# One set of convolution taps, another W_in order, and W_out through the SyncE ring

## The chip, the cores and the metric

One NeuronCore of one Trainium2 chip runs the whole program. The metric is device microseconds of one execution, lower is better. Each time is a median of several executions, with their lowest and highest value. "The span" is the length of the one execution that the profiler recorded, without the launch; times inside an execution count from the span's start. A "station" is the time of a named event in it, such as the first W_out matmul; a transfer has "landed" when its last completion signal arrives.

## The reference

A lightweight causal convolution (7 taps per head, softmax over the taps), followed by a feed-forward block with exact GELU:

```python
x: (8, 4096, 192) fp32, weight: (8, 7)         # 8 heads of 24 channels
w = softmax(weight, axis=-1)
y[b, s, 24*h + g] = sum_k w[h, k] * x[b, s - 6 + k, 24*h + g]   # zero before s = 0
x2 = y.reshape(32768, 192)
out = gelu(x2 @ w_in) @ w_out                   # (192, 2048), then (2048, 192)
```

## The kernel before

The 32768 tokens are two halves of 16384; half 0 lives on partitions 0 to 63, half 1 on 64 to 127. A "third" is 64 of the 192 channels (every third channel), so three thirds side by side hold a token's channels. Tiles are of 256 tokens per half at first (six of them), then of 512. A tile is loaded and transposed on VectorE; tiles 0 and 1 are convolved on TensorE (diagonal matrices times a bf16 copy of x), later tiles on VectorE. Then TensorE does x times W_in, ScalarE the GELU, and TensorE, one tile behind, GELU times W_out. The W_in work is done in units: the matmuls of one unit feed one GELU, and a slice of W_out matmuls stands between two units. The "halo" is the six tokens before a tile, which the convolution needs and GpSimd copies.

Cut to what the change touches (cuts marked):

```python
# GpSimd: identity mask first, then W_in in three pieces with a cast to bf16
g.wait_ge(S_MSET, 1)
... affine_select -> idb ...
for i in range(3):
    win_in(FP[i], FP[i + 1], S_WIN[i])
... halo(0) ...
g.dma_start(wout, W_out).then_inc(S_WOUT, 16)     # one transfer, casts to bf16
halo(1)

# VectorE: taps and diagonals, one set for each third
v.tensor_copy(wch, wnt with each head repeated 24 times)
for q in range(4):
    v.transpose(wcol[quarter q], wch ...)         # 32 x 96
def diag(p): v.tensor_tensor(dg[third p], idb, wcol[third p], ALU.mult)
diag(0); diag(1)                                  # third 2 is made on ScalarE
for p in range(NP): trans(0, p)                   # tile 0
dup(0)                                            # copy a W_in piece to the other 64 partitions
conv_out(v, 0, 1); conv_out(v, 0, 4)
dup(1); dup(2)
for p in range(NP): trans(1, p)                   # tile 1
for p in range(NP): cast(1, p)                    # fp32 -> bf16 for TensorE

# ScalarE
a.wait_ge(S_WARM, 1)                              # VectorE's memset of the warm-up tile
a.activation(out=hot, in_=warm, func=AF.Exp)
load(a, 0, (2, 3))                                # half of tile 0 of x
... softmax ...
for k in range(KS): a.activation(out=dg[third 2, tap k], in_=idb, func=AF.Copy, scale=wcol)
for p in range(NP): a.activation(out=xTb[0], in_=xT[0], func=AF.Copy)   # bf16 copy of tile 0

# TensorE
for i in range(16): t.matmul(hp[1], warm, warm)   # warm-up
... convolution of tile 0, then of tile 1 behind units 4 and 5 of tile 0 ...

# SyncE
load weight; load(sp, 0, (0, 1))                  # the other half of tile 0 of x
sp.wait_ge(S_WIN[0], 32)
load(sp, 1); load(sp, 2)
sp.wait_ge(S_WOUT, 16); load(sp, 3)
```

Of the kernel before, what the change touches and what calls it, by code (L numbers as in the profile page):

```python
# [11 lines left out]
def bass_lightweight_conv__then__act_gelu_exact_kernel(  # L12
# [36 lines left out]
    HX = 8  # L49
# [36 lines left out]
    CH = []  # L86
    for s in range(4):
        CH += [2 * s, 2 * s + 1, NF // 2 + 2 * s, NF // 2 + 2 * s + 1]
# [21 lines left out]
    with es:  # L110
# [9 lines left out]
        wch = sbt("wch", [32, D], F32)  # L120
        wcol = sbt("wcol", [128, NP * 32], F32)
        idb = sbt("idb", [128, 64], BF16)
        dg = sbt("dg", [128, NP * KS * 64], BF16)
# [14 lines left out]
        S_WOUT = sem("S_WOUT")  # L138
# [13 lines left out]
        S_DGA = sem("S_DGA")  # L152
# [55 lines left out]
        FP = [0, FQ, 2 * FQ, FH]  # L208

# [163 lines left out]
        def _(g):  # L373
# [6 lines left out]

            g.wait_ge(S_MSET, 1)
# [11 lines left out]
            for i in range(3):  # L393
                win_in(FP[i], FP[i + 1], S_WIN[i])

            def halo(n):
# [45 lines left out]
            g.dma_start(  # L442
                ap(wout, 0, [[NF * C, 128], [2 * C, NF // 2], [1, 2 * C]]),
                ap(woutt, 0, [[2 * C, 128], [256 * C, NF // 2], [1, 2 * C]]),
            ).then_inc(S_WOUT, 16)
            halo(1)
            for n in range(2, NB):
                halo(n)

        @block.vector  # L450
        def _(v):
# [16 lines left out]

            v.wait_ge(S_PRO, 4)
            v.transpose(wnt[:, :], wnm[:, :]).then_inc(S_PRO)  # L470
            v.wait_ge(S_PRO, 5)
            v.tensor_copy(
                ap(wch, 0, [[D, 32], [GRP, H], [1, GRP]]),
                ap(wnt, 0, [[32, 32], [1, H], [0, GRP]]),
            ).then_inc(S_PRO)
            v.wait_ge(S_PRO, 6)
            for q in range(4):
                v.transpose(
                    ap(wcol, 32 * q * NP * 32, [[NP * 32, 32], [1, NP * 32]]),
                    ap(wch, DQ * (q % 2), [[D, 32], [1, NP], [NP, 32]]),  # L480
                ).then_inc(S_PRO)
            v.wait_ge(S_PRO, 10)
            v.wait_ge(S_IDN, 2)

            def diag(p):
                v.tensor_tensor(
                    ap(dg, p * KS * 64, [[NP * KS * 64, 128], [64, KS], [1, 64]]),
                    ap(idb, 0, [[64, 128], [0, KS], [1, 64]]),
                    ap(wcol, p * 32, [[NP * 32, 128], [1, KS], [0, 64]]),
                    ALU.mult,  # L490
                ).then_inc(S_DG)
# [17 lines left out]

            def cast(n, p):  # L510
                v.wait_ge(S_TR, NP * n + p + 1)
                v.tensor_copy(
                    ap(xTb[PC[n]], p * XB + HX, [[NP * XB, 128], [1, WS[n]]]),
                    ap(xT[n % 2], p * XW + HX, [[NP * XW, 128], [1, WS[n]]]),
                ).then_inc(S_CAST[PC[n]])
# [21 lines left out]
            def conv(n, k, p):  # L537
# [13 lines left out]
                wk = wcol[:, p * 32 + kt : p * 32 + kt + 1]  # L551
# [30 lines left out]
            diag(0)  # L582
            diag(1)
            for p in range(NP):
                trans(0, p)
            dup(0)
            conv_out(v, 0, 1)
            conv_out(v, 0, 4)
            dup(1)
            dup(2)  # L590
            for p in range(NP):
                trans(1, p)
            for p in range(NP):
                cast(1, p)
# [21 lines left out]
        def _(a):  # L616
            a.wait_ge(S_WARM, 1)
            a.activation(out=hot[:, 0:1], in_=warm[0:1, 0:1], func=AF.Exp).then_inc(S_ACTP)
# [10 lines left out]
            a.activation(out=hot[:, 1:2], in_=warm[0:1, 0:1], func=AF.Gelu).then_inc(S_HOT)  # L629
            a.wait_ge(S_PRO, 10)  # L630
            a.wait_ge(S_IDN, 2)
            for k in range(KS):
                d0 = ((NP - 1) * KS + k) * 64
                c0 = (NP - 1) * 32 + k
                a.activation(
                    out=dg[:, d0 : d0 + 64],
                    in_=idb[:, :],
                    func=AF.Copy,
                    scale=wcol[:, c0 : c0 + 1],
                ).then_inc(S_DGA)  # L640
# [288 lines left out]
```

## Time and profile before

| | before |
|---|---|
| time, median of 3 runs | 684.32 us (683.9 to 684.7) |
| span of the profiled run | 682.0 us |
| TensorE busy | 676.2 us (99%) |
| VectorE / ScalarE / GpSimd busy | 82% / 79% / 5% |
| first W_out matmul | 19.24 us |
| from that matmul to the end | 662.8 us |

### The profile page before, as it was taken

The numbers are of one execution on the slowest core, as the hardware profiler recorded it, in microseconds if no ns is written. First come the engines' busy times: TensorE is split into PE (matmuls) and PEld (weight loads), VectorE is DVE, ScalarE is ACT, GpSimd is POOL, SyncE is SP. The second block draws the span as 40 slices with busy tenths as digits, with TensorE's granted clock in tenths as the row PEclk, the third lists the DMA queues.
The fourth block names the chain that finished last, engine by engine and source line by source line (L and its number), as shares of the span: only waits on it lengthen the run. The fifth ranks groups of instructions, "written<-read, shape, count | busy, mean of one in ns | idle before, by whom it ended". The sixth has DMA issues, their size and how long they took to land.

```text
span 682.0 us, 27319 instructions
## 1 busy us (share of the span) xinstructions
PE 676.2 (99%) x12576; PEld 407.5 (60%) x12576; DVE 562.2 (82%) x909; ACT 538.4 (79%) x557; POOL 35.1 (5%) x51
## 2 busy tenths in 40 slices
PE   8999999999999999999999999999999999999998
PEld 4899655555555555555555555555555555555556
DVE  7899979888889888899888898888898888988611
ACT  7899988777787777787777788777778777778772
POOL 4026100000000000000000000000000000000000
PEclk9999999999999999999999999999999999999999
DMA  9345322134432143332234322334422434310223
GB/s 178 77 107 130 83 60 72 44 78 95 95 94 54 45 94 94 95 77 52 63 94 95 94 68 45 80 94 96 94 53 46 95 94 96 82 43 21 48 49 94
DMA packets 132946, 54.00 MB, mean 79 GB/s; under 512 B 126432, under 2 KB 132704, under 8 KB 132832
## 3 DMA queue, kind: packets, MB, share of 16 engines
q1 hardware_dynamic: 129872, 49.93, 31.5%
q0 software_dynamic: 2288, 1.57, 1.6%
q8 instruction: 98, 1.61, 1.0%
q10 hardware_dynamic: 672, 0.76, 0.4%
q14 instruction: 16, 0.13, 0.1%
HBM read 28.66 MB, written 25.17 MB: 79 GB/s over the span
## 4 chain that ended last, share of the span: by engine, by line
PE 97%; ACT 2%; issue 0%; DVE 0%
PE hp L774 47%; PE ob L838 43%; PE ob L805 6%; ACT gT L694 2%; PE hp L708 1%; PE ob L727 0%; ACT xc L192 0%; ACT osb L261 0%; DVE osb L303 0%; DVE osb L272 0%; DVE warm L452 0%
## 5 line engine op out<-in xcount | busy, mean ns | idle before, releaser
L694 ACT ACTIVATE gT<-hp 128x1024 bf16<-128x1024 f32 x512 | 522.8, 1023 | 129.3 <-PE hp L774 126.0
L774 PE MATMUL hp<-xc,win 64*64 64x512 bf16 (+2 forms) x6048 | 418.9, 366 | 1.5 <-ACT gT L694 0.7
L838 PE MATMUL ob<-gT,wout 64*64 64x512 bf16 x5376 | 366.3, 376 | 0.0
L561 DVE SCALAR_TENSOR_TENSOR acc<-xT,wcol,acc 128x512 f32<-128x512 f32 (+1 forms) x495 | 314.6, 700 | 0.5 <-ACT acc L667 0.5
L774 PEld LDWEIGHTS hp<-xc,win 64*64 64x64 bf16 (+1 forms) x6048 | 187.7, 106 | 136.3 <-ACT gT L694 2.5
L838 PEld LDWEIGHTS ob<-gT,wout 64*64 64x64 bf16 x5376 | 172.2, 118 | 122.9
L303 DVE STREAM_TRANSPOSE osb<-ob 128x512 f32<-128x512 f32 x84 | 74.2, 886 | 100.8 <-PE ob L838 100.8
L528 DVE STREAM_TRANSPOSE xT<-xin 128x512 f32<-128x512 f32 (+1 forms) x105 | 78.7, 803 | 2.1 <-DMA xin<-in_x_dram 2.1
L561 DVE SCALAR_TENSOR_TENSOR xc<-xT,wcol,acc 128x512 bf16<-128x512 f32 (+1 forms) x99 | 65.3, 717 | 0.0
L438 POOL COPY xT<-xT 128x18 f32<-128x18 f32 x30 | 27.9, 930 | 515.3 <-DVE xT L528 492.3
L805 PE MATMUL ob<-wout,gT 64*128 64x192 bf16 x1024 | 52.2, 243 | 0.3
L805 PEld LDWEIGHTS ob<-wout,gT 64*128 64x128 bf16 x1024 | 43.5, 94 | 6.4 <-PE ob L805 0.6
L554 DVE TENSOR_SCALAR acc<-xT,wcol 128x512 f32<-128x512 f32 (+1 forms) x90 | 37.6, 474 | 1.1
L274 ACT ACTIVATE osb<-ob 128x192 f32<-128x192 f32 x4 | 1.3, 330 | 9.5 <-PE ob L805 9.5
L272 DVE COPY osb<-ob 128x192 f32<-128x192 f32 x4 | 1.4, 357 | 8.4 <-PE ob L805 8.4
L708 PE MATMUL hp<-warm 128*128 128x512 bf16 x16 | 6.3, 581 | 1.3 <-DVE warm L452 1.3
L261 ACT ACTIVATE osb<-ob 128x384 f32<-128x384 f32 x12 | 5.8, 487 | 0.0
L667 ACT ACTIVATE acc<-xT,wcol 128x256 f32<-128x256 f32 (+1 forms) x9 | 5.2, 575 | 0.0
L708 PEld LDWEIGHTS hp<-warm 128*128 128x128 bf16 x16 | 2.1, 139 | 4.9 <-issue 3.6
L194 DVE CAST xc<-ob 64x256 bf16<-64x256 f32 (+3 forms) x8 | 2.8, 358 | 1.6 <-PE ob L727 1.4
L376 POOL DMA_DIRECT2D win<-in_moe_w_in_dram x6 | 3.9, 653 | 0.0
L497 DVE COPY win<-win 64x768 bf16<-64x768 bf16 (+1 forms) x6 | 3.1, 509 | 0.2
(33 smaller groups left out, 21.7 us busy)
## 6 DMA issues: line engine op xcount, KB each, us to landing
out_dram<-osb SPq DMA_DIRECT2D x122, 192.0 KB, 3.1
xin<-in_x_dram SPq DMA_DIRECT2D x116, 192.0 KB, 4.1
xin<-in_x_dram SPq DMA_DIRECT2D x20, 96.0 KB, 3.2
wout<-in_moe_w_out_dram POOLq DMA_DIRECT2D x1, 768.0 KB, 11.0
win<-in_moe_w_in_dram POOLq DMA_DIRECT2D x4, 96.0 KB, 4.2
win<-in_moe_w_in_dram POOLq DMA_DIRECT2D x2, 192.0 KB, 4.8
out_dram<-osb SPq DMA_DIRECT2D x8, 48.0 KB, 1.7
out_dram<-osb ACTq DMA_DIRECT2D x4, 96.0 KB, 1.9
```

The costliest lines, as they stand in the source:

```text
L261: e.activation(out=dst, in_=src, func=AF.Copy).then_inc(S_EVA)
L303: v.transpose(ap(osb[m % 2], j, [[8 * C, 128], [C // 2, TB // 32], [NP, 32]]), bank(ring(m, j)),).then_inc(S_EV)
L438: g.tensor_copy(dst, src).then_inc(S_HALO)
L528: v.transpose(ap(xT[n % 2], p * XW + HX, [[NP * XW, 128], [1, w]]), ap(xin[n % NX], p, [[TB // 32 * DQ, 128], [D if n == 0 else DQ, w // 3 ...
L554: ins = v.tensor_scalar(a, src, wk, None, ALU.mult)
L561: ins = v.scalar_tensor_tensor(dst, src, wk, a, op0=ALU.mult, op1=ALU.add)
L667: a.activation(out=acc[n % 2][:, p * TB : p * TB + w], in_=ap(xT[n % 2], p * XW + HX, [[NP * XW, 128], [1, w]]), func=AF.Copy, scale=wcol[ ...
L694: a.activation(out=ap(gT[n % 2], i * c * 2 * w, dst), in_=ap(hp[u % 2], 0, src), func=AF.Gelu,).then_inc(S_GELU)
L708: t.matmul(hp[1][:, 0:512], warm[:, 0:128], warm[:, :])
L774: ins = t.matmul(hp[u % 2][fo : fo + fw, o : o + w], ap(win, f1, [[NP * F, 64], [2, fw]]), xc[n % 2][r, p * TB : p * TB + w], start=(p == ...
L805: ins = t.matmul(bank(bb[sub], w=C), gT[m % 2][r, c0 : c0 + 128], wout[r, CH[i] * C : (CH[i] + 1) * C], start=(ph == 0 and i == 0), stop=( ...
L838: ins = t.matmul(bank(ring(m, j), slice(64 * h, 64 * h + 64), w), ap(wout, 64 * hf * NF * C + CH[i] * C + j, [[NF * C, 64], [NP, 64]],), g ...
```

## The change

The intent is to shorten the start. One set of taps and diagonals for all thirds (a head has 24 channels, a multiple of 3, so channel number j of every third belongs to the same head), each token half begins with its own part of W_in, and W_out comes as fp32 in the SyncE ring and is cast on GpSimd. The diff cut to its core:

```diff
 # taps: the channel order lets all thirds use one column set
-    v.tensor_copy(wch ...); 4 x v.transpose(32 x 96); diag(0); diag(1); 7 ScalarE products
+    4 x v.transpose(32 x 32); 1 x v.tensor_tensor(dg, idb, wcol)

 # ScalarE: the first activation no longer reads the warm-up tile
-    a.wait_ge(S_WARM, 1)
-    a.activation(out=hot[:, 0:1], in_=warm[0:1, 0:1], func=AF.Exp)
+    a.activation(out=hot[:, 0:1], in_=const zero, func=AF.Exp)
     load(a, 0, (2, 3))

 # W_in order: half hf uses W_in chunks 8*hf, 8*hf+1, ... so its own partitions come first
-    CH = [0, 1, 8, 9, 2, 3, 10, 11, ...]          # the same for both halves
+    CH = [[(8 * hf + i) % NF for i in range(NF)] for hf in range(2)]
-    if n == 0 and i in (0, 2, 4): wait S_WIN[i // 2] and S_DUPE >= 2 * (i // 2) + 2
+    if n == 0 and i < 3:      wait S_WIN[i]
+    if n == 0 and 4 <= i < 7: wait S_DUPE >= 2 * (i - 4) + 2

 # GpSimd: first W_in piece ahead of the identity mask; casts move here
+    win_in(FP[0], FP[1], S_WIN[0])
     ... identity mask ...
-    for i in range(3): win_in(...)
+    for i in range(1, 3): win_in(...)
     halo(0)
-    g.dma_start(wout <- W_out, cast).then_inc(S_WOUT, 16)
     halo(1)
+    for p in range(NP): cast(g, 1, p)             # was on VectorE
+    for i in range(4):
+        g.wait_ge(S_WOUT[i], 16)
+        g.tensor_copy(wout[quarter i], woutf[quarter i]).then_inc(S_WOG)

 # SyncE
     load(sp, 1)
+    for i in range(4): sp.dma_start(woutf[quarter i] <- W_out).then_inc(S_WOUT[i], 16)
     load(sp, 2)
-    sp.wait_ge(S_WOUT, 16)
     load(sp, 3)

 # VectorE: conv_out(0) before dup(0); dup(2) after the transposes of tile 1
 # TensorE: share of W_out work behind tile 1's units: [3, 4, 4, ...] -> [4, 8, 8, 8, 9, ...]
```

More of the change, by code (lines that the diff above doesn't have):

```diff
@@ L81, in bass_lightweight_conv__then__act_gelu_exact_kernel @@
         EVC.append(EVC[n] + (0 if n < NA else NP if new else NG[n]))
-    CH = []
-    for s in range(4):
-        CH += [2 * s, 2 * s + 1, NF // 2 + 2 * s, NF // 2 + 2 * s + 1]
+    CH = [[(8 * hf + i) % NF for i in range(NF)] for hf in range(2)]
     assert all(WS[n] == TB for n in range(M0, NB))
@@ L119, in bass_lightweight_conv__then__act_gelu_exact_kernel @@
         wnt = sbt("wnt", [32, 32], F32)
-        wch = sbt("wch", [32, D], F32)
-        wcol = sbt("wcol", [128, NP * 32], F32)
+        wcol = sbt("wcol", [128, 32], F32)
+        woutf = sbt("woutf", [128, NF * C], F32)
         idb = sbt("idb", [128, 64], BF16)
-        dg = sbt("dg", [128, NP * KS * 64], BF16)
+        dg = sbt("dg", [128, KS * 64], BF16)
         warm = sbt("warm", [128, 512], BF16)
@@ L137, in bass_lightweight_conv__then__act_gelu_exact_kernel @@
         S_WIN = [sem("S_WIN%d" % i) for i in range(3)]
-        S_WOUT = sem("S_WOUT")
+        S_WOUT = [sem("S_WOUT%d" % i) for i in range(4)]
+        S_WOG = sem("S_WOG")
         S_XIN = [sem("S_XIN%d" % i) for i in range(NX)]
@@ L151, in bass_lightweight_conv__then__act_gelu_exact_kernel @@
         S_PCA = sem("S_PCA")
-        S_DGA = sem("S_DGA")
         S_DUPE = sem("S_DUPE")
@@ L208, in bass_lightweight_conv__then__act_gelu_exact_kernel, with cast @@
         FP = [0, FQ, 2 * FQ, FH]
+        WG = [0, 4, 2, 6]
+        def cast(e, n, p):
+            e.wait_ge(S_TR, NP * n + p + 1)
+            e.tensor_copy(
+                ap(xTb[PC[n]], p * XB + HX, [[NP * XB, 128], [1, WS[n]]]),
+                ap(xT[n % 2], p * XW + HX, [[NP * XW, 128], [1, WS[n]]]),
+            ).then_inc(S_CAST[PC[n]])
         def cvd(n):
@@ L392, in _ @@
                 ).then_inc(S_IDN)
-            for i in range(3):
+            for i in range(1, 3):
                 win_in(FP[i], FP[i + 1], S_WIN[i])
@@ L441, in _ @@
             halo(0)
-            g.dma_start(
-                ap(wout, 0, [[NF * C, 128], [2 * C, NF // 2], [1, 2 * C]]),
-                ap(woutt, 0, [[2 * C, 128], [256 * C, NF // 2], [1, 2 * C]]),
-            ).then_inc(S_WOUT, 16)
             halo(1)
+            for p in range(NP):
+                cast(g, 1, p)
+            for i in range(4):
+                g.wait_ge(S_WOUT[i], 16)
+                o = 2 * WG[i] * C
+                g.tensor_copy(wout[:, o : o + 4 * C], woutf[:, o : o + 4 * C]).then_inc(S_WOG)
             for n in range(2, NB):
@@ L471, in _ @@
             v.wait_ge(S_PRO, 5)
-            v.tensor_copy(
-                ap(wch, 0, [[D, 32], [GRP, H], [1, GRP]]),
-                ap(wnt, 0, [[32, 32], [1, H], [0, GRP]]),
-            ).then_inc(S_PRO)
-            v.wait_ge(S_PRO, 6)
             for q in range(4):
                 v.transpose(
-                    ap(wcol, 32 * q * NP * 32, [[NP * 32, 32], [1, NP * 32]]),
-                    ap(wch, DQ * (q % 2), [[D, 32], [1, NP], [NP, 32]]),
+                    wcol[32 * q : 32 * q + 32, :],
+                    ap(wnt, 4 * (q % 2), [[32, 32], [1, 4], [0, 8]]),
                 ).then_inc(S_PRO)
-            v.wait_ge(S_PRO, 10)
+            v.wait_ge(S_PRO, 9)
             v.wait_ge(S_IDN, 2)
-            def diag(p):
-                v.tensor_tensor(
-                    ap(dg, p * KS * 64, [[NP * KS * 64, 128], [64, KS], [1, 64]]),
-                    ap(idb, 0, [[64, 128], [0, KS], [1, 64]]),
-                    ap(wcol, p * 32, [[NP * 32, 128], [1, KS], [0, 64]]),
-                    ALU.mult,
-                ).then_inc(S_DG)
+            v.tensor_tensor(
+                ap(dg, 0, [[KS * 64, 128], [64, KS], [1, 64]]),
+                ap(idb, 0, [[64, 128], [0, KS], [1, 64]]),
+                ap(wcol, 0, [[32, 128], [1, KS], [0, 64]]),
+                ALU.mult,
+            ).then_inc(S_DG)
             def dup(s):
@@ L508, in dup @@
                     ).then_inc(S_DUPE)
-            def cast(n, p):
-                v.wait_ge(S_TR, NP * n + p + 1)
-                v.tensor_copy(
-                    ap(xTb[PC[n]], p * XB + HX, [[NP * XB, 128], [1, WS[n]]]),
-                    ap(xT[n % 2], p * XW + HX, [[NP * XW, 128], [1, WS[n]]]),
-                ).then_inc(S_CAST[PC[n]])
             def trans(n, p):
@@ L550, in conv @@
                 src = ap(xT[n % 2], p * XW + HF + kt, [[NP * XW, 128], [1, w]])
-                wk = wcol[:, p * 32 + kt : p * 32 + kt + 1]
+                wk = wcol[:, kt : kt + 1]
                 a = acc[n % 2][:, p * TB : p * TB + w]
@@ L580, in run @@
                     conv(*op[1:])
-            diag(0)
-            diag(1)
             for p in range(NP):
                 trans(0, p)
-            dup(0)
             conv_out(v, 0, 1)
             conv_out(v, 0, 4)
+            dup(0)
             dup(1)
-            dup(2)
             for p in range(NP):
                 trans(1, p)
-            for p in range(NP):
-                cast(1, p)
+            dup(2)
             for j in range(len(PIECES)):
@@ L616, in _ @@
         def _(a):
-            a.wait_ge(S_WARM, 1)
-            a.activation(out=hot[:, 0:1], in_=warm[0:1, 0:1], func=AF.Exp).then_inc(S_ACTP)
+            a.activation(
+                out=hot[:, 0:1], in_=nc.const_aps.tensor(0.0, (1, 1), F32), func=AF.Exp
+            ).then_inc(S_ACTP)
             load(a, 0, (2, 3))
@@ L628, in _ @@
             ).then_inc(S_ACTP)
-            a.activation(out=hot[:, 1:2], in_=warm[0:1, 0:1], func=AF.Gelu).then_inc(S_HOT)
-            a.wait_ge(S_PRO, 10)
-            a.wait_ge(S_IDN, 2)
-            for k in range(KS):
-                d0 = ((NP - 1) * KS + k) * 64
-                c0 = (NP - 1) * 32 + k
-                a.activation(
-                    out=dg[:, d0 : d0 + 64],
-                    in_=idb[:, :],
-                    func=AF.Copy,
-                    scale=wcol[:, c0 : c0 + 1],
-                ).then_inc(S_DGA)
+            a.activation(
+                out=hot[:, 1:2], in_=nc.const_aps.tensor(0.0, (1, 1), F32), func=AF.Gelu
+            ).then_inc(S_HOT)
+            a.wait_ge(S_PRO, 9)
             for p in range(NP):
@@ L670, in first_tap @@
                     func=AF.Copy,
-                    scale=wcol[:, p * 32 + KS - 1 : p * 32 + KS],
+                    scale=wcol[:, KS - 1 : KS],
                 ).then_inc(S_K0)
@@ L715, in pconv @@
                     if n == 0:
-                        if p < NP - 1:
-                            t.wait_ge(S_DG, p + 1)
-                        else:
-                            t.wait_ge(S_DGA, KS)
+                        t.wait_ge(S_DG, 1)
                 if k == KS - 2:
@@ L724, in pconv @@
                     r = slice(64 * hf, 64 * hf + 64)
-                    d0 = (p * KS + k) * 64
+                    d0 = k * 64
                     x0 = p * XB + (32 * k if n == 0 else HF + k) + c0
@@ L759, in mm1 @@
                         t.wait_ge(S_CV, cvd(n))
-                if n == 0 and i in (0, 2, 4):
-                    t.wait_ge(S_WIN[i // 2], 32)
-                    t.wait_ge(S_DUPE, 2 * (i // 2) + 2)
+                if n == 0 and i < 3:
+                    t.wait_ge(S_WIN[i], 32)
+                if n == 0 and 4 <= i < 7:
+                    t.wait_ge(S_DUPE, 2 * (i - 4) + 2)
                 for cc in range(c):
-                    f0 = 256 * (CH[i * c + cc] // 2) + CH[i * c + cc] % 2
                     for p in range(NP):
@@ L769, in mm1 @@
                             r = slice(64 * hf, 64 * hf + 64)
+                            ch = CH[hf][i * c + cc]
+                            f0 = 256 * (ch // 2) + ch % 2
                             fw = 64 if M0 < n <= M1 else 128
@@ L807, in mm2 @@
                         gT[m % 2][r, c0 : c0 + 128],
-                        wout[r, CH[i] * C : (CH[i] + 1) * C],
+                        wout[r, CH[sub][i] * C : (CH[sub][i] + 1) * C],
                         start=(ph == 0 and i == 0),
@@ L814, in mm2 @@
                     ins.then_inc(S_MM2 if ph == 1 else S_PH)
-            share = {1: [3, 4, 4, 4, 4, 4, 4, 4]}
+            share = {1: [4, 8, 8, 8, 9, 9, 9, 9]}
             def mm2_t(m, ps, i):
@@ L841, in mm2_t @@
                                 wout,
-                                64 * hf * NF * C + CH[i] * C + j,
+                                64 * hf * NF * C + CH[h][i] * C + j,
                                 [[NF * C, 64], [NP, 64]],
@@ L872, in _ @@
                     a1 = len(todo) * sum(ws[: i + 1]) // sum(ws)
-                    if n == 1 and a0 == 0 and a1 > 0:
-                        t.wait_ge(S_WOUT, 16)
                     for un in todo[a0:a1]:
+                        if n == 1 and un in ((0, 0, 0), (0, 0, 4)):
+                            t.wait_ge(S_WOG, 2 + un[2] // 2)
                         (mm2_t if new else mm2)(n - 1, *un)
@@ L889, in _ @@
             load(sp, 1)
+            for i in range(4):
+                g = WG[i]
+                sp.dma_start(
+                    ap(woutf, 2 * g * C, [[NF * C, 128], [2 * C, 2], [1, 2 * C]]),
+                    ap(woutt, 256 * g * C, [[2 * C, 128], [256 * C, 2], [1, 2 * C]]),
+                ).then_inc(S_WOUT[i], 16)
             load(sp, 2)
-            sp.wait_ge(S_WOUT, 16)
             load(sp, 3)
```

## The prediction

0.09 + 0.08, about 0.2 us, and 0.2 for an early clock bring 684.3 to 683.9. The second 0.2 was the author's estimate: the profile of before shows one time at which the warm-up becomes fast, 6.8 us. That W_in's first piece could hold up x of tile 0 by 0.7 us is an estimate too. It assumes that the piece gets half the turns, which was not shown: the trace of before has W_in's packets from 4.85 us on, the last of x until 5.55 us (the 5.2 and 5.9 of the prediction), and those x packets take 0.32 to 0.42 us each, the earlier ones of the same queue 0.22 to 0.41. That VectorE could shut GpSimd out rests on the one copy of 3.56 us.

> **What bounds the kernel now.** I read the chain that ended last first, since it says which engine a saved microsecond has to come from.
>
> ```profile
> PE 97%; ACT 2%; issue 0%; DVE 0%
> PE hp L774 47%; PE ob L838 43%; PE ob L805 6%; ACT gT L694 2%; PE hp L708 1%; PE ob L727 0%; ACT xc L192 0%; ACT osb L261 0%; DVE osb L303 0%; DVE osb L272 0%; DVE warm L452 0%
> ```
>
> TensorE is the path for 97% of a 682.0 us span; GELU on ScalarE is there for 2%, VectorE for nothing. The two big matmul groups (x times W_in, GELU times W_out) are 90%. To see where the rest lies I took busy time by stretch. In 30 to 350 us TensorE is busy 319.87 of 320.00 us, in 350 to 670 us 319.85 of 320.00. From 18.5 to 30 us it is 11.36 of 11.50. So nothing after 18.5 us can be won by removing a wait; the change touches no matmul count or shape there. What is left is the start, so I read the chain in order of time (start us, length us, what):
>
> ```profile
> 1.26 6.32 PE hp L708 x16
> 7.58 0.90 PE ob L727 x22
> 8.48 0.02 issue
> 8.50 0.38 ACT xc L192
> ...
> 9.94 0.63 PE hp L774 x8
> 10.57 0.02 issue
> 10.59 1.94 ACT gT L694 x2
> 12.53 0.01 issue
> 12.54 1.03 ACT gT L694
> 13.57 0.05 issue
> 13.62 0.83 PE hp L774 x12
> 14.45 0.89 PE ob L727 x28
> ...
> 17.43 1.03 ACT gT L694
> 18.46 0.05 issue
> 18.51 0.83 PE hp L774 x12
> 19.34 0.58 PE ob L805 x12
> ```
>
> This is the whole argument. The start is a relay: 16 warm-up matmuls (to 7.58), the convolution of tile 0 on TensorE, four copies on ScalarE (8.50 to 9.89), then eight GELUs of about 1.02 us, which bound the stretch from 10.59 to 19.48 us together with the convolution of tile 1 that sits between them. From the seventh GELU's end (18.46) the matrix engine runs without a break. A microsecond counts only if that moment, or the wait just after it, moves.
>
> The diagonal, tap and transpose work on VectorE is beside the warm-up, as its timeline shows (start, busy us, engine, line):
>
> ```profile
> 3.68 0.25 DVE L472 COPY wch<-wnt 32x192 f32<-32x192 f32 x1
> 3.96 1.28 DVE L478 STREAM_TRANSPOSE wcol<-wch 32x96 f32<-32x96 f32 x4
> 5.28 1.16 DVE L486 TENSOR_TENSOR dg<-idb,wcol 128x448 bf16<-128x448 bf16 x2
> 6.36 1.34 DVE L528 STREAM_TRANSPOSE xT<-xin 128x256 f32<-128x256 f32 x3
> ```
>
> [...] the warm-up matmuls start 0.427 us apart until 6.77 us, then 0.216 us apart; the last is issued at 7.20 and is done about 7.42. [...] this point may move between executions, which is part of the noise. [...] in the trace the GpSimd packets begin at 5.2 us while the last x packets of tile 0 are still going (they end at 5.9)[...]. [...] a GpSimd copy of 128x18 takes 0.22 to 0.31 us alone, but the one that begins at 39.37 us, in a run of scalar_tensor_tensor, took 3.56 us.
>
> **The change, part by part.**
>
> *One set of taps and diagonals.* Removed on VectorE: the 0.28 us wch step (3.68 to 3.96). Four transposes of 32x96 in 1.28 us become 32x32; the one of that size at 3.45 took 0.20, so about 0.8 for four. One of the two 0.58 us diagonal products goes. Sum: 0.28 + 0.48 + 0.58 = 1.3 us, so VectorE could transpose tile 0 at about 5.0 instead of 6.36. Seven ScalarE products (1.78 us, ending about 7.06) go too. But the packets of x for tile 0 end at 5.93, so the transpose begins at about 6.05 at best: 0.3 us won there. From the first transpose to the first convolution matmul took 7.51 - 6.36 = 1.15 us, so TensorE could begin at 7.2. The warm-up holds it until about 7.42. Of 1.3 us saved only 7.51 - 7.42 = 0.09 us reaches the path. The convolution's own pace (0.107 us per tap) and ScalarE's four copies behind it stay.
>
> *Each half begins with its own W_in.* The duplicates are now needed at the fifth unit instead of the first. In the kernel before, the first duplicates (7.73 to 8.60) were already done before the first GELU matmul at 9.34, so this frees nothing on the path; worth 0. The second and third pieces of W_in are wanted at units 1 and 2 (10.6 and 11.7 us); their packets ended at 7.98 and 10.07, so no new wait. W_in's first issue moves ahead of the identity mask, from 1.83 to about 0.8 us, as GpSimd waited there for VectorE. That lets tile 1 of x be issued about 0.9 us earlier (it waits for that piece)[...].
>
> *W_out through SyncE.* In the kernel before it was issued at 8.17 on GpSimd, took 11.0 us, and landed at 19.2: exactly when TensorE wanted it. The first W_out weight load at 19.24 is put down to that DMA. The switch cost 19.24 - 18.51 = 0.73 us where the next such one cost 20.40 - 19.75 = 0.65: 0.08 us lost, which the change wins back. The new transfers sit behind tile 1 in the ring, so with about 0.45 us per issue they start near 8 to 10 us. The source bytes are unchanged; a 768-byte-out packet took 84 ns, 1024 of them over 16 engines 5.4 us, so all should land by 15 to 16. Casts on GpSimd, estimated: a 128x186 cast took 0.34 and a 128x18 one 0.22, so 0.7 ns per element, and 0.75 us for 128x768 undisturbed; scaling the slowest (0.457 for 186) gives 1.9. Two casts are wanted at 19.2, all four at 20.5. With tile 1's casts done by about 13.5 even four slow ones end at 21; with normal ones, 17. I take them as in time.
>
> *Tile 1's cast from VectorE to GpSimd.* About 0.4 to 0.6 us each for 128x256 instead of 0.22. The convolution of tile 1 cannot issue before the third GELU ends (13.57) and the fifth unit's matmuls are done (14.45). If tile 1 of x lands nearer 11 than 12.2, the casts end by 13.5. Hidden.
>
> *Fewer W_out units in tile 1's first slice.* The same 64, moved later; GELU has slack there. Zero.
>
> Sum: 0.09 + 0.08 = about 0.2 us on the path out of 684.3. I add 0.2 for executions where the clock rises earlier, so that the full shortening of VectorE's prologue (up to 0.3) shows: 683.9 us.
>
> **The rivals.** *x of tile 0 becomes the wait.* W_in's packets now begin near 4.2 instead of 5.2[...]. If W_in's first piece (384 packets of 60 ns, 1.4 us over 16 engines) gets half the turns, x lands up to 0.7 us later, at about 6.6, and the convolution begins at 7.8: 0.3 us slower than now, 684.6. Against it: single x packets of 0.35 to 0.4 us grew no longer while W_in ran beside them. *GpSimd is late.* If VectorE's duplicates and convolution shut it out, the casts or the halo of tile 2 behind them slip; TensorE would wait at 20 us or for tile 2's convolution at about 29.8. VectorE ends that at 28.77, only 1 us ahead. For: the 3.56 us copy. Against: tile 2's x arrives sooner without the old W_out beside it (VectorE idled 1.72 us for it until 19.39), and the long two-input series begins only at 21.56. That would cost 1 to 2 us: 685 to 686. *The whole 1.3 us shows.* Only if warm-up were not the limit; then 683.0. The chain's first piece speaks against it.
>
> **Range and chances.** The three runs span 0.8 us, the net effect lies between -1.0 and +0.7 in most cases: 683.0 to 684.9. A 2% step is 13.7 us, more than the entire ramp before steady state could give, and no late wait could cost that: faster 0.005, same 0.985, slower 0.01.
>
> **What would show it.** Warm-up still first in the chain, with the first convolution matmul at 7.4 to 7.5 and the first GELU at 10.5; the seventh GELU ending near 18.4; VectorE's tile 0 transposes waiting for the x DMA; no W_out wait at the first W_out matmul, and GpSimd's four casts ended by 19. Wrong if a convolution matmul waits for a GpSimd cast, if W_out's matmuls wait for GpSimd, or if TensorE's steady pace after 30 us differs.

## The result, and the profile after

The changed kernel took 683.62 us (683.38 to 684.2, 4 runs); the kernel before, with one run more, 684.11 us (683.87 to 684.7, 4 runs). The ratio is 0.9993 with a 95% interval of 0.9976 to 1.001. A ratio here is the mean time of one kernel's fast runs over the mean of the other's fast runs of the same rounds, so not quite the ratio of the two medians. The forecast, 683.9 in 683.0 to 684.9, holds, and an effect of this size is not resolved from the scatter by the timed runs alone. Repeated on another chip with five rounds (run c1) it was 683.58 against 683.75 us, ratio 0.9998 (0.9985 to 1.001): there the medians differ by 0.17 us, not 0.49.

The profiles are finer than the timer here. The chain that ended last, in order of time, of the changed kernel (start us, length us, what):

```profile
1.64 4.27 DMA xin<-in_x_dram
...
5.93 0.53 DVE xT L526
...
6.55 0.43 ACT xTb L630
...
7.02 0.97 PE ob L711 x18
...
8.01 0.39 ACT xc L191
...
10.10 1.94 ACT gT L681 x2
...
16.93 1.03 ACT gT L681
...
18.01 0.83 PE hp L760 x12
18.84 0.33 PE ob L791 x8
```

Set beside the chain of before, every station from the first GELU to the last lies 0.49 or 0.50 us earlier: 10.10 for 10.59, 16.93 for 17.43, 18.01 for 18.51. The chain now starts with the loading of x and goes through VectorE's transpose and ScalarE's cast; the warm-up is no longer on it. VectorE in the same stretch (start, busy us, engine, line, in brackets the idle time before and what ended it):

```profile
3.69 0.90 DVE L485 STREAM_TRANSPOSE wcol<-wnt 32x32 f32<-32x32 f32 x4
4.62 0.63 DVE L491 TENSOR_TENSOR dg<-idb,wcol 128x448 bf16<-128x448 bf16 x1
5.93 1.33 DVE L526 STREAM_TRANSPOSE xT<-xin 128x256 f32<-128x256 f32 x3 [0.68 <-DMA xin<-in_x_dram]
```

The taps now end at 5.25 us and VectorE stands idle 0.68 us for x. The three tap rows of before ended at 6.44.

The first W_out matmul came 0.56 us earlier (18.68 for 19.24), but the span fell by 0.43 us (682.04 to 681.61, to two decimals from the packed traces): the rest is given back later. From the first W_out matmul to the end it is 662.93 us, against 662.80 before. The place is tile 2; the chain of before, then that of the changed kernel:

```profile
29.76 0.66 PE hp L774 x12
```

```profile
29.22 0.79 PE hp L760 x12
...
30.67 0.65 PE hp L760 x12
```

The first W_in unit of tile 2 (29.22) takes 0.79 instead of the 0.65 of the next: I put this down to VectorE, whose convolution of tile 2 began late (next fence) and ended at 29.03, because x of tile 2 landed at 19.62 us (19.36 before); a2 below names the wait.

```profile
19.65 1.35 DVE L526 STREAM_TRANSPOSE xT<-xin 128x256 f32<-128x256 f32 x3 [1.54 <-DMA xin<-in_x_dram]
...
27.77 1.26 DVE L559 SCALAR_TENSOR_TENSOR xc<-xT,wcol,acc 128x256 bf16<-128x256 f32 x3
```

W_out came in time. GpSimd's rows show its four casts, after tile 1's three (13.00 to 14.47), the last of them waiting for its transfer:

```profile
14.41 2.56 POOL L457 CAST wout<-woutf 128x768 bf16<-128x768 f32 x3
18.22 0.83 POOL L457 CAST wout<-woutf 128x768 bf16<-128x768 f32 x1 [1.25 <-DMA woutf<-in_moe_w_out_dram]
```

They end at 19.05; the second slice of W_out matmuls, which needs the last two, starts at 19.70.

Why did x of tile 0 land earlier, at 5.91 instead of 6.33 us (times of the last completion signal in the trace)? ScalarE's queue, before and after, answers it; the pair of loads is the second half of tile 0:

```profile
1.25 0.88 ACTq L321 DMA_DIRECT2D xin<-in_x_dram  x2
```

```profile
0.88 0.86 ACTq L329 DMA_DIRECT2D xin<-in_x_dram  x2
```

The dropped wait for the warm-up memset let ScalarE issue them 0.37 us earlier. The packets agree: in the kernel before ScalarE's were the last of tile 0's, ending at 5.55; in the changed kernel they end at 4.18 and SyncE's are the last, at 5.11. I had not counted that line of the diff at all.

### The profile page after: what moved, and what is told of

Read it like the earlier page. It is cut to its first block, busy times and chain, and to the rows that moved or that the text cites. A ratio compares the mean times of both kernels' runs of the same rounds, so it can differ in the third digit from the quotient of the medians.

```text
span 681.6 us, 27317 instructions
## 1 busy us (share of the span) xinstructions
PE 675.0 (99%) x12576; PEld 410.1 (60%) x12576; DVE 561.0 (82%) x904; ACT 537.3 (79%) x550; POOL 38.9 (6%) x57
## 4 chain that ended last, share of the span: by engine, by line
PE 96%; ACT 2%; DMA 1%; issue 0%; DVE 0%; SPq 0%; ACTq 0%
PE hp L760 48%; PE ob L824 43%; PE ob L791 6%; ACT gT L681 2%; DMA xin<-in_x_dram 1%; PE ob L711 0%; ACT xc L191 0%; ACT osb L269 0%; DVE osb L311 0%; DVE xT L526 0%; ACT xTb L630 0%; SPq L872 0%; DVE osb L280 0%; SPq L329 0%; ACTq L629 0%
## 5 line engine op out<-in xcount | busy, mean ns | idle before, releaser
L760 PEld LDWEIGHTS hp<-xc,win 64*64 64x64 bf16 (+1 forms) x6048 | 189.9, 106 | 134.8 <-ACT gT L681 2.5
L791 PEld LDWEIGHTS ob<-wout,gT 64*128 64x128 bf16 x1024 | 44.9, 94 | 5.2 <-PE ob L791 0.6
L711 PE MATMUL ob<-xTb,dg 64*64 64x256 bf16 (+1 forms) x112 | 3.2, 245 | 0.7 <-ACT xTb L630 0.7
```

The source lines that it names most:

```text
L760: ins = t.matmul(hp[u % 2][fo : fo + fw, o : o + w], ap(win, f1, [[NP * F, 64], [2, fw]]), xc[n % 2][r, p * TB : p * TB + w], start=(p == ...
L791: ins = t.matmul(bank(bb[sub], w=C), gT[m % 2][r, c0 : c0 + 128], wout[r, CH[sub][i] * C : (CH[sub][i] + 1) * C], start=(ph == 0 and i == ...
```

## The experiments

Theory after reading the traces: the start is set by two things together, x of tile 0 (6.33 before) and VectorE's taps (6.36 before), which in the kernel before happen to end at the same moment; the change moves both. Rivals: the taps alone; the earlier load alone; or merely a clock that rose early in the profiled run. The warm-up differs from one execution to the next: its matmuls became fast (0.216 us apart instead of 0.427) at 6.8 us in the profile of before and at 4.2 us in that of after, so in the second they had long ended when the convolution was ready. Over all 14 profiles the warm-up matmuls, which begin at 1.26 us, became fast after 6 slow ones at 4.1 us at the earliest (a2) and after 14 at 7.2 us at the latest (b4), about 3 us apart; in a3 and a4 all 12 were slow. In experiments a1 to a4 I therefore shortened the warm-up from 16 to 12 matmuls, so that it ends by about 6.4 us at either clock (1.26 + 12 x 0.427; an estimate from the profile of before).

All kernels gave the correct result. The stations, worked out from each packed trace (us; one profile of each kernel; the last column is the span minus the first W_out matmul):

| kernel | x of tile 0 landed | first convolution matmul | tile 1's convolution | first W_out matmul | span | rest |
|---|---|---|---|---|---|---|
| before | 6.33 | 7.51 | 14.38 | 19.24 | 682.04 | 662.80 |
| after | 5.91 | 7.02 | 13.89 | 18.68 | 681.61 | 662.93 |
| a1 | 6.19 | 7.41 | 15.19 | 19.98 | 682.73 | 662.75 |
| a2 | 5.96 | 7.07 | 13.94 | 18.73 | 681.87 | 663.14 |
| a3 | 6.92 | 8.02 | 14.89 | 19.68 | 682.45 | 662.77 |
| a4 | 5.94 | 7.42 | 14.29 | 19.08 | 681.86 | 662.78 |
| b1 | 5.93 | 7.50 | 14.37 | 19.16 | 683.78 | 664.62 |
| b2 | 6.58 | 7.69 | 14.56 | 19.36 | 683.81 | 664.45 |
| b3 | 5.92 | 7.04 | 14.17 | 19.16 | 681.92 | 662.76 |
| b4 | 5.93 | 7.71 | 14.58 | 19.37 | 682.13 | 662.76 |
| c1 | 5.82 | 7.29 | 14.42 | 19.61 | 682.60 | 662.99 |
| c2 | 5.97 | 7.09 | 14.17 | 19.54 | 682.30 | 662.76 |
| c3 | 5.97 | 7.09 | 13.96 | 18.86 | 681.65 | 662.79 |
| c4 | 5.88 | 6.99 | 13.86 | 18.84 | 681.62 | 662.78 |

"Rest" is 662.75 to 662.80 wherever nothing waits later, whatever was done to the start. So a microsecond at the first W_out matmul is a microsecond of the span, and a larger rest marks a later wait.

**a1, the kernel before with 12 warm-ups.**

```diff
-            for i in range(16):
+            for i in range(12):
                 t.matmul(hp[1][:, 0:512], warm[:, 0:128], warm[:, :])
```

> The kernel before with 12 warm-up matmuls instead of 16, so that the warm-up ends by about 6.4 us even at the slow clock (1.26 + 12 x 0.427). If the first convolution matmul of the kernel before waits for the tile-0 transpose and its cast (my theory now), it stays at 7.5 us and the time stays at 684.1, with less scatter. If the warm-up set it, as my prediction had it, the matmul comes earlier and the time falls by up to 0.1 us.

Measured: 684.50 us (683.57 to 684.54, 5 runs) beside 683.63 for the kernel before (683.59 to 683.75, 9 runs, same chip), ratio 1.0008 (0.9995 to 1.002). The first convolution matmul came at 7.41 instead of 7.51. Here VectorE's taps and ScalarE's seven products (until 7.05) and cast bind it; so in the profile of before the warm-up was the last to end, but only by 0.10 us, with these two close behind: the matmul moved by what the rival forecast allowed, and no further. But the scatter grew, against my expectation, with three of the five runs at 684.5 us: in the profiled one of these the warm-up became fast at 4.1 us and ended near 5.4, TensorE then idled 2.04 us, and the clock fell back. The table by stretch shows it (the granted clock is the column PEclk):

```profile
core 0: us, PE busy (x) PEld busy (x) DVE busy (x) ACT busy (x) POOL busy (x), PEclk, DMA share, GB/s
5.00:8.00 3.00, 0.96 (x12) 0.56 (x14) 2.94 (x7) 2.73 (x10) 1.85 (x6) 0.90 1.30 176
8.00:11.00 3.00, 3.00 (x64) 2.41 (x58) 1.68 (x5) 1.43 (x5) 1.29 (x3) 0.53 1.20 223
```

From 8 to 11 us the clock was 0.53 of full, and tile 0's convolution took 2.81 us instead of 1.63. The three runs at 684.5 us all list a granted clock of 0.998, the other two 1.0. Only this one profile shows such a fall: after a gap of 1.73 us in a2 the convolution took 1.69 us. In the eight profiles with 16 warm-ups the longest gap before the convolution was 0.71 us (the changed kernel), so I take the extra four for insurance against a long gap; how long it may be was not shown.

**a2, the changed kernel with 12 warm-ups.** The same edit.

> The changed kernel with 12 warm-up matmuls. Theory: first convolution matmul at 7.0 us in every execution, since neither clock phase can hold it, and 683.5 us, 0.4 to 0.5 under the kernel before with 12. Rival (the gain seen in the profile was only a lucky early clock): no difference between the two kernels with 12 warm-ups.

Measured: 683.53 us (683.17 to 683.63, 5 runs), ratio to the kernel before 0.9997 (0.9984 to 1.0009). The convolution began at 7.07, the first W_out matmul at 18.73, with a warm-up too short to hold them, so the earlier start is not only an accident of the clock. I expected 0.4 to 0.5 us under a1; it was 0.97, but most of that is a1's clock. Against the kernel before it is 0.10 us by the medians. The span was 681.87, because 0.34 us was given back (663.14 against 662.80), and this time the profile names it:

```profile
29.42 0.83 PE L760 MATMUL hp<-xc,win 64*128 64x256 bf16 x12 [0.18 <-DVE xc L559]
```

TensorE waits for VectorE's convolution of tile 2. x of tile 2 landed at 19.87 in this run. What is won at the start is lost there: the fair partner, a4 below (the kernel before with 12 warm-ups and no fall of the clock), began its convolution 0.35 us later and has the same span, 681.86.

**a3, the changed kernel, 12 warm-ups, with ScalarE's wait put back.**

```diff
+            a.wait_ge(S_WARM, 1)
             a.activation(out=hot[:, 0:1], in_=const zero, func=AF.Exp)
             load(a, 0, (2, 3))
```

> The changed kernel with 12 warm-ups and ScalarE's wait for the warm-up memset put back before its two loads of x. Theory: those loads are issued 0.37 us later, tile 0 of x lands near 6.3 instead of 5.9, the first convolution matmul goes back to about 7.4, and nearly all of the gain (0.4 us) is lost although all the tap savings stay. Rival (the taps alone made the gain): 7.0 and 683.5 as without the wait.

Measured: 683.69 us (683.59 to 684.18, 5 runs), ratio 1.0001 (0.9989 to 1.0014). In the profile:

```profile
4.61 0.63 DVE L491 TENSOR_TENSOR dg<-idb,wcol 128x448 bf16<-128x448 bf16 x1
6.94 1.34 DVE L526 STREAM_TRANSPOSE xT<-xin 128x256 f32<-128x256 f32 x3 [1.71 <-DMA xin<-in_x_dram]
```

The taps end at 5.24 as before, x does not land until 6.92, and the convolution begins at 8.02: 0.95 us later than in a2, and later than in the kernel before. I expected 6.3 and 7.4. The extra 0.6 us I put down to the earlier W_in packets (from 3.92 us, against 4.85 in the kernel before): ScalarE's late x packets now run beside them (they lasted until 6.27 us, against 5.55). That would be the first rival of the prediction at nearly the size I gave it (0.7), which the change would escape because its own ScalarE loads go out ahead of W_in (from 0.88 us, W_in from 1.32). It is one profile: in b2, with W_in's packets from 4.00 and ScalarE's loads later still, x landed at 6.58, so the size is not shown.

**a4, the kernel before, 12 warm-ups, without that wait.**

```diff
-            a.wait_ge(S_WARM, 1)
-            a.activation(out=hot[:, 0:1], in_=warm[0:1, 0:1], func=AF.Exp)
+            a.activation(out=hot[:, 0:1], in_=const zero, func=AF.Exp)
```

> The kernel before with 12 warm-ups and without that wait on ScalarE. Theory: x lands near 5.9, but VectorE is at the diagonals until about 6.4, so the transpose stays at 6.36 and the time at 684.1: each half alone gives nothing. Rival (the earlier load alone makes the gain): first convolution matmul at 7.0 and 683.6.

Measured: 683.61 us (683.6 to 684.05, 5 runs), ratio 1.0001. x landed at 5.94, yet the transpose stayed where it was, behind the diagonals:

```profile
5.28 1.16 DVE L486 TENSOR_TENSOR dg<-idb,wcol 128x448 bf16<-128x448 bf16 x2
6.36 1.32 DVE L528 STREAM_TRANSPOSE xT<-xin 128x256 f32<-128x256 f32 x3
```

a3 and a4 together: the taps without the earlier load win nothing, the earlier load without the taps wins nothing (7.42 here, 7.41 in a1), both together move the convolution from 7.4 to 7.1 with 12 warm-ups (a2). The taps alone in the kernel before, with W_in late, were not run; its x at 6.33 and the 1.1 us from landing to convolution in the changed kernel, a2 and a3 give 7.4, an estimate that agrees. All this is read from stations; by the timer a1 to a4 are not told apart from the kernel before.

**b1, the changed kernel with x of tile 2 ahead of half of W_out.** If tile 2 limits, its x should come earlier.

```diff
             load(sp, 1)
             for i in range(4):
+                if i == 2:
+                    load(sp, 2)
                 sp.dma_start(woutf[quarter i] ...)
-            load(sp, 2)
```

> The changed kernel with the loads of tile 2 of x ahead of the last two of the four W_out transfers in SyncE's ring. Theory (the new W_out traffic delays x of tile 2 to 19.6 us, so that VectorE's convolution of tile 2 ends at 29.0, at or after the time TensorE wants it): x of tile 2 lands near 17, VectorE begins it at about 18.1 and ends by 27.6, TensorE has no wait at tile 2; the late W_out halves land near 19.5 and their casts end near 20.3, so up to 0.5 us may be lost at the second W_out slice instead. Net -0.2 to +0.4 us against the changed kernel. Rival (tile 2 does not matter): same tile-2 picture and no change.

Measured: 685.08 us (684.52 to 685.52, 5 runs) beside 683.70 (683.55 to 685.41, 11 runs), ratio 1.0017 (1.0005 to 1.0029): slower, by more than I allowed for. x of tile 2 landed at 17.87 as expected, but the last two W_out quarters only at 19.26 and 21.05 (I had said 19.5 for both), and TensorE stood still for their casts:

```profile
21.99 0.83 PE L791 MATMUL ob<-wout,gT 64*128 64x192 bf16 x16 [1.68 <-POOL wout L457]
```

Nor did tile 2 gain: VectorE waited 1.40 us for the halo of tile 2, which GpSimd copies after these casts, and ended its convolution at 29.33 (29.03 in the changed kernel). So the ring has no slack: W_out's last quarter is wanted at 19.7 and tile 2's x near 19.4 (an estimate from the 19.36 of before, which held nothing up), and whichever goes last is late. The author's order is the better of the two tried.

This profile shows one thing more. Its clock rose as late as in the profile of before (last warm-up matmul issued at 7.19 and 7.20), x of tile 0 had landed at 5.93, and yet:

```profile
1.26 6.31 PE L695 MATMUL hp<-warm 128*128 128x512 bf16 x16 [1.26 <-DVE warm L463]
7.50 1.38 PE L711 MATMUL ob<-xTb,dg 64*64 64x256 bf16 x56
```

The convolution began at 7.50, against 7.51 in before: with a clock that late the warm-up hides everything that the change wins at the start.

**b2, the same, with the tap weights' load moved to ScalarE's queue ahead of its x loads, and 14 warm-ups.** This was meant to bring x of tile 0 still earlier.

```diff
-            sp.dma_start(wsb ...).then_inc(S_WSB, 16)      # SyncE
             ...
+            a.dma_start(wsb ...).then_inc(S_WSB, 16)       # ScalarE, before load(a, 0, (2, 3))
```

> The same and the tap weights' small load moved from SyncE to ScalarE's queue, so that SyncE's two loads of x for tile 0 are issued at 0.8 instead of 1.27 us; 14 warm-ups. Theory (x of tile 0 is what starts the relay in the changed kernel): x lands near 5.5, first convolution matmul near 6.6, first GELU near 9.7, a further 0.3 to 0.4 us off unless W_out or tile 2 of x then holds TensorE at 20 or 29 us, which would show as a wait there. Rival (VectorE's taps hold it): stays at 7.0.

Measured: 685.36 us (684.6 to 688.73, 6 runs), ratio 1.0035 (1.0014 to 1.0055). A miss. The tap weights arrived so late from that queue that the first tap instruction on VectorE ran at 3.62 instead of 2.17 us and the taps ended at 6.70; ScalarE's x loads, behind them, landed at 6.58. The convolution went back to 7.69, and b1's loss came on top.

**b3, the kernel before with the taps and the dropped wait, nothing else.**

```diff
 (the taps and ScalarE parts of the change; W_in order, W_out path and tile 1's casts as before)
```

> The kernel before with only two parts of the change: one set of taps and diagonals, and no wait of ScalarE before its x loads. W_in order and W_out path as before. Theory: first convolution matmul at 7.0 when the clock rises early, as in the changed kernel; W_out, landing at 18.5 to 19.2, is then wanted at 18.75 and TensorE waits up to 0.4 us for it, so 0.1 to 0.5 us under the kernel before. Rival (the W_in order carries the gain): 7.4 or later and nothing gained.

Measured: 683.70 us (683.35 to 683.92, 5 runs), ratio 0.9997 (0.9985 to 1.0009). The convolution of tile 0 began at 7.04, as in the changed kernel: W_in's order has no part in that. But W_out was not what took the gain back; it landed at 18.2, before it was wanted. Tile 1 took it:

```profile
12.60 1.34 DVE L519 STREAM_TRANSPOSE xT<-xin 128x256 f32<-128x256 f32 x3 [0.85 <-DMA xin<-in_x_dram]
13.86 0.66 DVE L503 CAST xTb<-xT 128x256 bf16<-128x256 f32 x3
```

x of tile 1 lands at 12.58 and all three transposes come before the first cast, so tile 1's convolution started at 14.17 and its first half took 1.16 us in the chain instead of 0.89; of 0.47 us gained at tile 0, 0.02 was left at the W_in unit before the first W_out matmul (18.49 for 18.51), and 0.08 at that matmul (19.16 for 19.24), since it no longer waited for W_out. The cast that I had filed as hidden became the next wait.

**b4, the changed kernel with W_in behind the mask again.**

```diff
-            win_in(FP[0], FP[1], S_WIN[0])
             g.wait_ge(S_MSET, 1)
             ... mask ...
-            for i in range(1, 3):
+            for i in range(3):
```

> The changed kernel with the first W_in transfer issued after the identity mask again, as in the kernel before. Theory (early W_in packets compete with x of tile 0): x lands near 5.5 instead of 5.9 and the first convolution matmul comes at about 6.7, or as soon as the warm-up lets it (6.9 to 7.4); x of tile 1, which waits for that W_in piece, is issued up to 0.5 us later. Net within 0.2 us. Rival (no competition): x still lands at 5.9.

Measured: 683.61 us (683.18 to 684.27, 5 runs), ratio 0.9997. x of tile 0 landed at 5.93, not 5.5: with ScalarE's loads early, W_in's start does not matter to it, and my theory fails for this kernel (a3, where those loads were late, fits it). The test itself was weak, since W_in's first packets moved only from 4.48 to 4.56 us; but in c1 they began at 4.09 and x landed at 5.82. In the profiled run the clock rose only at 7.2 us, the last warm-up matmul was issued at 7.40, and that held the convolution until 7.71. So even here the warm-up decides in some executions: in three (b1, b4, c1) of the seven profiles with 16 warm-ups, the short taps and the early load. In these three, as in before, the convolution begins 0.31 us after the last warm-up matmul is issued.

**c1, the changed kernel again.** No edit.

> The changed kernel itself again, beside the variants. Both theories: 0.1 to 0.5 us under the kernel before, depending on when the clock rises; ratio 0.9993 to 0.9999.

Measured: 683.58 us (683.34 to 684.37, 5 runs) beside 683.75 (683.58 to 685.06, 9 runs), ratio 0.9998. The profiled run was the slowest of the five: the warm-up held the convolution until 7.29, x of tile 1 landed at 13.35 (12.39 in the first profile of this kernel), and the first W_out matmul came at 19.61. My reading, from this one profile: the kernel has traded fixed work for dependence on when transfers land.

**c2, the changed kernel with tile 1's casts back on VectorE.**

```diff
-            for p in range(NP):
-                cast(g, 1, p)
 ...
                 trans(1, p)
+            for p in range(NP):
+                cast(v, 1, p)
             dup(2)
```

> The changed kernel with tile 1's three casts back on VectorE, after its three transposes. Theory (the earlier start is only kept because GpSimd casts each third as soon as it is transposed; x of tile 1 lands at 12.4 whatever the start): the first cast ends about 0.5 us later, the convolution of tile 1 starts at 14.2 instead of 13.9, and the first W_out matmul comes 0.3 us later, near 19.0 to 19.1 when the clock rose early. Rival (the cast is hidden, as my prediction had it): no change.

Measured: 684.08 us (683.96 to 684.97, 5 runs), ratio 1.0007 (0.9995 to 1.002); in the same rounds the changed kernel had 683.58. The convolution of tile 1 began at 14.17, as expected, and a second loss followed, since VectorE's last W_in duplicates now come after the casts:

```profile
14.17 1.15 PE L711 MATMUL ob<-xTb,dg 64*64 64x256 bf16 x28
...
16.85 1.49 PE L760 MATMUL hp<-xc,win 64*128 64x256 bf16 x24 [0.25 <-DVE win L500]
```

First W_out matmul at 19.54, 0.86 later than in the changed kernel and later than in the kernel before. Not all of it is the cast's place: the duplicates stand behind it, and GpSimd's casts of W_out now ran beside VectorE's work (the first cast took 0.64 us, the other two 0.28). What the place alone is worth, b3 and c3 show.

**c3, the kernel before with taps, dropped wait and tile 1's casts on GpSimd.**

```diff
 (b3, and: )
-            for p in range(NP): cast(1, p)        # VectorE
+            for p in range(NP): cast(g, 1, p)     # GpSimd, after halo(1)
```

> The kernel before with one set of taps, no wait of ScalarE before its x loads, and tile 1's casts on GpSimd; W_in order and W_out path as before. Theory: these three carry the gain; first W_out matmul at 18.8 to 19.0 when the clock rose early (19.32 without the GpSimd casts), x of tile 2 at 18.4 leaves TensorE no wait at tile 2, so equal to the changed kernel or up to 0.2 us under it. Rival (W_in order or the W_out path is needed): TensorE waits for W_out near 18.7 or for a W_in duplicate, and the time is that of the kernel before.

Measured: 683.68 us (683.38 to 683.85, 5 runs), ratio 0.9997 (0.9985 to 1.001). The profile, with a span of 681.6 us, has the changed kernel's gain without its W_in order and without its W_out path: tile 1's convolution at 13.96, the first W_out matmul at 18.86, no wait at tile 2 (x of tile 2 landed at 18.89). W_out landed at 18.72, just in time. b3 differs from it only in who casts tile 1, and x of tile 1 landed alike in both (12.58 and 12.59): the cast's place moved tile 1's convolution by 0.21 us and the first W_out matmul by 0.30.

**c4, c3 with 13 warm-ups.**

> The same with 13 warm-ups, which end by 6.8 us even at the slow clock. Theory: convolution at 7.0 in every execution, so 683.3 with little scatter. Rival (shorter warm-up lets the clock fall back in the gap, as one run with 12 showed): scattered, 0.5 to 1 us slower in some executions.

Measured: 683.49 us (683.27 to 684.03, 5 runs), ratio 0.9997 (0.9984 to 1.0011). The convolution began at 6.99. The scatter did not shrink, so the expectation of "little scatter" failed; what scatters besides the clock (c1 suggests the landing of x of tile 1) I did not separate. Here W_out, landing at 18.8, did hold TensorE a little: the chain gives 0.67 us to the first 12 W_out matmuls, 0.50 in c3. No version tried beats the changed kernel by more than the scatter.

## Why the prediction was right or wrong

The outcome was right: 683.9 forecast, 683.62 measured, and "same" as good as certain. That the number agrees so well is luck: the forecast was 0.2 us by the sum and 0.2 us for an early clock, the profiled spans fell by 0.43 us, and two of the terms in that, the dropped wait and the loss at tile 2, were not in the sum. By its steps:

**The bound.** Right. TensorE is saturated after the start; "rest" was 662.75 to 662.80 us in every kernel without a later wait. Nothing changed in the steady part.

**"the packets of x for tile 0 end at 5.93, so the transpose begins at about 6.05 at best: 0.3 us won there".** The number came true (5.93 in the changed kernel) for a wrong reason. I had read the packet records with an origin 0.37 us too early; on the span's clock the last x packet ends at 5.55, and the completion signal comes 0.78 later, at 6.33. So in the kernel before x itself held the transpose, together with the taps. (The taps end 1.19 us earlier, 5.25 for 6.44, against the 1.3 forecast.) Shortening VectorE alone wins nothing (a3 without the early load, a4 for the reverse). What moved x to 5.91 is a line of the diff that I did not price, the dropped wait ahead of ScalarE's loads. The same slip makes the other packet times in the prediction (W_in ending at 7.98 and 10.07, GpSimd's packets from 5.2) 0.37 us too late; W_out's 19.2, taken from the issue and its landing, is not affected.

**"only 7.51 - 7.42 = 0.09 us reaches the path"**, plus 0.2 for executions with an early clock. The mechanism is right, the sizes were off. With the clock of before, b1 shows 7.50 for 7.51, so 0.01: the warm-up holds the convolution until 7.51, not 7.42. With an early clock the convolution came at 7.02; of the 0.49 between the two profiles 0.10 is the clock alone (a1 and a4 have 7.41 and 7.42 without a warm-up that holds them), and about 0.39 is the change, against the 0.2 to 0.3 forecast. Nine traces of kernels with the earlier load and the short taps put the convolution between 6.99 and 7.71.

**W_in's order: 0.** W_in's first issue came at 1.32 us, not at the 0.8 I had put down, and its first packets moved at 4.48, 3.2 us after the issue began (in before 4.85, 3.0 us after an issue begun at 1.83, which took 0.79), with x being loaded on the other queues; tile 1 of x was issued 0.4 us earlier (6.53 for 6.93), not 0.9. The worth is right as far as tested: b3 and c3 reach the same start without it, and c3 the same span (681.65 against 681.61), though its first W_out matmul is 0.18 later (18.86). It was tested only together with the old W_out path and the old share of W_out work, so what each is worth inside the changed kernel is open.

**W_out: 0.08 us.** The wait is gone. The landing estimate was too early (18.17 for the last quarter instead of 15 to 16), and the cast took 0.83 us against an estimated 0.75; they ended at 19.05 instead of 17, and the margin to 19.70 was 0.65 us. b1 showed how thin that is.

**Tile 1's cast: "Hidden."** This step failed. Its premise did: x of tile 1 landed at 12.39, not nearer 11 (12.18 before), and the three casts ended at 14.47, not 13.5. It is hidden only where it now stands: back on VectorE it costs the gain (c2), and without it most of the shorter start is lost at tile 1 (b3 against c3, 0.30 us). The error was to test the old position against the old times. Once tile 0 starts 0.5 us earlier and x of tile 1 does not, the cast becomes the next thing on the path.

**The rivals.** x of tile 0 competing with W_in fits a3 (landed at 6.92) and did not show here (5.91). GpSimd's casts shut out by VectorE did not happen (the four of W_out took 0.83 to 1.02 us each); rather VectorE was slower: its copy of 64x1536 took 1.28 us beside GpSimd's casts of W_out, 0.69 in before, and ended at 15.78, in time for the unit at 16.13. The rival's other half, tile 2, did, for another reason than stated: I argued that "tile 2's x arrives sooner"; it arrived at 19.62 instead of 19.36, behind fp32 W_out in the same ring, and TensorE gave back 0.13 us in that profile and 0.34 in a2.

So the two profiles differ by 0.10 from the clock, 0.39 from the change at the first convolution (both conditions, early clock), kept to the W_out matmuls by the cast's move, 0.07 from the W_out wait (19.24 to 18.68 is 0.56), minus 0.13 at tile 2: 0.43, the difference of the two spans. Without the clock's part it is 0.33, and in an execution with a clock as late as that of before nearly nothing is left of the 0.39.

## What to carry to other kernels

When two inputs of a step end within a few hundredths of a microsecond of each other, shortening either one alone is worth nothing (here x at 6.33 and the taps at 6.36: a3 and a4); look for the second (and here a third, the warm-up) before pricing the first, and price every line of the diff, a dropped wait ahead of a transfer included. After moving a station earlier, check each later station against its own transfer at the new time. Before calling the difference of two profiles a gain, see whether the clock rose at the same time in both (here at 6.8 and 4.2 us). When a profile's stations and one constant remainder explain the span, compare those, and let the timer only decide whether it matters.
